# A recurrent attention step and a gated two-layer product on one core: four f-tiles in three passes, paired gates, a step's decays as products, another order

## The chip, the cores and the metric

The kernel runs on one core of a Trainium2 chip. The time is that of the device for one execution, in microseconds (us). Five engines run side by side, each through its own list of instructions in order: TensorE (PE, matrix products), VectorE (DVE), ScalarE (ACT), GpSimd (POOL) and SyncE (SP), which mostly issues transfers. They wait for each other by semaphores.

## What is computed

```python
for t in range(S):                      # B, H, S, D = 4, 8, 768, 48
    kt, vt, rt = (k[:, :, t], v[:, :, t], r[:, :, t])
    cur = np.einsum('bhd,bhe->bhde', u[None] * kt, vt)
    y[:, :, t] = np.einsum('bhd,bhde->bhe', rt, state + cur)
    state = w[None, :, :, None] * state + np.einsum('bhd,bhe->bhde', kt, vt)
x = y.transpose(0, 2, 1, 3).reshape(B * S, H * D)      # 3072 tokens x 384
h = x @ w_in                                           # w_in 384 x 2048
g = h * np.tanh(softplus(h))
out = g @ w_out                                        # w_out 2048 x 384
```

All of it is in float32.

## The kernel before

**Attention.** The recurrence is computed in 24 steps. A step takes 64 tokens of two of the four batches, so step s carries on the states of step s - 2. For each step, DVE multiplies r and k by powers of the decay w (`scale`), PE forms the scores within the 64 tokens (`scores`), DVE puts them under a mask (`attend`) into a tile P that holds on its diagonal the sums of r, u and k. PE then forms the outputs from the carried states and from P and v (`rows_y`), and the new states' additions from the keys (`keys`) and v. The states are multiplied by w to the 64th (`w64`) and added to what PE made (`update_state`): one scaling and two additions on DVE, or the scaling on ACT. The sums for the diagonal come from PE for the first steps (`N_SQ`, `N_PE`: two steps in one form, the steps up to the sixth in another, 32 rows each in the trace) and from three DVE instructions over the normal layout of r and k for the others (`dots`).

**The gated product.** Four steps make a group of 512 tokens; there are six groups, 0 to 5. The 2048 inner columns are 16 f-tiles of 128. For each f-tile PE forms `hp` (x times w_in), ACT or DVE copies it out of PSUM into `hb` (`evacuate`), two f-tiles make a batch of 1024 columns, and ACT runs three functions over it (`gate`: sigmoid, arctangent, sine into `fa`). The third needs another table than the first two, so each batch loads a table twice. DVE multiplies `hb` by the result (`mix`). PE multiplies the product with w_out into three accumulators.

**Two forms of a product.** The weights arrive as 64-bit numbers in 16 blocks (`wraw`) and are turned into float32 by one ACT and three DVE instructions each (`convert`). A float32 product in the plain form shows as two rows in the trace. In the other form a number is split into a high and a low part (type fp32r), for weights by `split` (one ACT and one DVE instruction over 768 columns), and three products are formed: high with high, high with low, low with high (`three`). All groups but 0 use three passes throughout. Group 0 uses the plain form until the weights have been split: its w_in tiles are worked in `UNITS`, first four units of two f-tiles for the first 256 tokens (steps 0 and 1), the same four for the other 256, and then f-tiles 8 to 15 one by one over 512 tokens. Only those last eight use three passes (`FROM` = 8), from a split copy of x (`xp`, made by `split_x`). The products with w_out in group 0 read the gated tile `gf` directly, plain, up to f-tile 13.

**What sets the order.** The program keeps a planner (`Flow`). Each piece of work is a generator that yields what it waits for and what it costs on one or several engines; the planner picks, by these costs, by ranks and by a table of numbers (`SHIFT`), the next piece, and so fixes each engine's list and, for pieces that two engines can do, the engine. On the chip each engine then runs its list in order.

Of the kernel before, what the change touches and what calls it, by code (L numbers as in the profile page):

```python
# [10 lines left out]
F32 = mybir.dt.float32  # L11
# [11 lines left out]
NP = H // 2  # L23
C = 128
# [40 lines left out]
N_SQ, N_PE = 2, 6  # L65
OWN = 3
CHECK_AT, CHECK_STEP = 44, 3
DIAG_ACT = (1, 2, 5, 6, 7, 10)
# [8 lines left out]
def first_use(c):  # L77
# [15 lines left out]
PAIRS = ()  # L93
BY_STEP = 0
FROM, FROM2 = 8, 14
X_SPLIT = 5
CONVERT = (639.144, -3157.076, -1693.42, -2376.477)
LAG = 8
AHEAD_LEAST, AHEAD_MOST, DOWN = 1, 8, 3
LO0, HI0, LO1, HI1 = 0.15, 0.5, 0.1, 0.5  # L100
LAT, LAT0 = 0.15, 0.13
WARM0, WARM_MIN, FILL = 10, 0.3, 0.28
# [9 lines left out]
RANK = dict(token_table=-1935.7, keys=466.6, first_state=-1349.0)  # L112
# [8 lines left out]
    attend10=-85.0, attend9=1.0, convert10=-3.0, convert11=-13.0, convert4=-75.0, convert6=70.0, convert8=-31.0,  # L121
    convert9=77.0, diag5=-21.0, dots10=-7.0, evacuate12=54.0, evacuate23=-33.0, evacuate27=-34.0, evacuate4=87.0,
    gate10=-55.0, gate11=-30.0, gate12=-2.0, gate2=-7.0, gate3=-45.0, gate5=17.0, gate9=-81.0, keys10=20.0,
    mix1=23.0, mix3=-52.0, outputs10=-2.0, outputs12=-8.0, outputs13=2.0, outputs4=-2.0, outputs6=-191.0,
    outputs7=15.0, outputs8=11.0, scale10=5.0, scale11=32.0, scale6=-3.0, scale7=-7.0, split13=-88.0,
# [3 lines left out]
class Flow:  # L129
# [127 lines left out]
def rwkv_mish_kernel(ctx, tc, rkT, rkN, vN, wT, w_in, w_out, consts, rkF, vF, wF, uF, outT):  # L257
# [71 lines left out]
    pre = work.tile([128, 2 * KT * 64], F32, name="pre", tag="fa", bufs=1)  # L329
# [453 lines left out]

    def rows_y(s, last):
# [50 lines left out]
        if not last:  # L835
            state_products(s, new_states(ys), False)
# [14 lines left out]
    def outputs(s):  # L851
# [26 lines left out]
        else:  # L878
            more = merged and with_sums(s + 1)
            yield pe(1.45 + 0.65 * merged - 0.4 * last + 0.27 * more, 192 + 64 * merged - 64 * last + 64 * more)  # L880
# [240 lines left out]
    def tile_cost(g, halved=False):  # L1121
        return pe(9 * (T + 33) / 2400, 18) if g else pe(3 * 4 * (T + 3) / 2400, 24 if halved else 12)

    def split_x():

        if FROM >= NF:
            return
# [3 lines left out]
        for k in range(KT):  # L1131
# [511 lines left out]
```

## Time and profile before

| | |
|---|---|
| median of 3 runs | 466.83 us (466.33 to 466.9) |
| profiled execution | 468.58 us, of which the span from the first to the last instruction is 466.7 us |
| PE busy | 455.4 us (98%) |
| DVE busy | 374.6 us (80%) |
| ACT busy | 392.4 us (84%) |
| DMA | 60.1 MB, 129 GB/s in the mean |

A row of the profile is a group of instructions or a single one with its start, its duration and, in brackets, how long its engine stood idle ahead of it and for whom. PE's matmuls overlap: a row of 512 columns is shown with 0.38 us, though the next starts 0.22 us later, so the spacing of starts is what one costs. PEld are the weight loads. DVE and ACT rows overlap by about 0.1 us in the same way.

### The profile page before, as it was taken

Reading aid. Unit: us, or ns where it says so; the run is one execution under the profiler, and the core shown is the slowest. Engines: PE = TensorE matmul, PEld = TensorE weight load, DVE = VectorE, ACT = ScalarE, POOL = GpSimd, SP = SyncE. Lnnn points to the kernel's source line nnn. Section 1 sums busy time; section 2 is a strip of 40 time slices with the busy share of each in tenths; the row PEclk is TensorE's granted clock in tenths of the full one; section 3 lists DMA queues with packets and bytes.
Section 4 is the critical chain, followed back from the end, with each engine's and each line's share of the span. In section 5 each row is a group of like instructions: output and inputs, shape, how many; then the busy total and the mean of one; then the engine's idle time right before and its main releaser. Section 6 shows DMA issues by size and latency. Waiting matters only on the chain.

```text
span 466.7 us, 11536 instructions
## 1 busy us (share of the span) xinstructions
PE 455.4 (98%) x4927; PEld 382.7 (82%) x4927; DVE 374.6 (80%) x594; ACT 392.4 (84%) x505; POOL 4.5 (1%) x31
## 2 busy tenths in 40 slices
PE   9899999999999999999999999999999999999995
PEld 5687888756888888888888888888888888888884
DVE  6899999999898989597986799986799575646661
ACT  5668897999999885897689978799979799989981
POOL 1000000000000000000000000000000000000000
PEclk9999999999999999999999999999999999999998
DMA  8866666612312331315351365242445040212001
GB/s 313 301 217 217 234 233 215 223 26 95 103 69 91 101 106 44 103 72 164 126 185 67 113 213 202 92 165 69 156 145 194 14 139 22 115 67 70 1 0 72
DMA packets 20168, 60.14 MB, mean 129 GB/s; under 512 B 3312, under 2 KB 4304, under 8 KB 20112
## 3 DMA queue, kind: packets, MB, share of 16 engines
q1 hardware_dynamic: 17664, 55.11, 34.9%
q10 hardware_dynamic: 2448, 4.25, 2.4%
q8 instruction: 39, 0.64, 0.6%
q14 instruction: 17, 0.14, 0.1%
HBM read 52.57 MB, written 4.72 MB: 123 GB/s over the span
## 4 chain that ended last, share of the span: by engine, by line
PE 57%; DVE 14%; DMA 12%; ACT 11%; SPq 2%; issue 2%; ACTq 0%; DVEq 0%
PE acc L360 27%; PE hp L360 27%; DMA wraw<-in_w_out_dram 5%; DMA wraw<-in_w_in_dram 3%; PE pa L360 2%; DMA first<-in_rkT_dram 2%; SPq L988 2%; ACT L1056 2%; DMA kn<-in_rkN_dram 2%; ACT fa L1056 1%; ACT fa L1062 1%; DVE hb L1072 1%; DVE gl L1080 1%; DVE rk L628 1%; ACT L1062 1%
## 5 line engine op out<-in xcount | busy, mean ns | idle before, releaser
L360 PE MATMUL hp<-x,w 128*128 128x512 f32 x720 | 164.8, 382 | 2.0 <-DVE hb L1265 1.5
L360 PEld LDWEIGHTS hp<-x,w 128*128 128x128 f32 x720 | 134.9, 189 | 22.4 <-DVE hb L1265 1.9
L360 PE MATMUL acc<-gh,w 128*128 128x512 f32 x492 | 152.8, 380 | 0.0
L360 PEld LDWEIGHTS acc<-gh,w 128*128 128x128 f32 x492 | 93.0, 189 | 13.5
L360 PE MATMUL acc<-gl,w 128*128 128x512 f32 x246 | 92.7, 379 | 0.0
L1072 DVE TENSOR_TENSOR hb<-hb,fa 128x1024 f32<-128x1024 f32 x40 | 48.9, 1222 | 33.9 <-ACT fa L1062 33.7
L1056 ACT ACT_TABLE_LOAD x47 | 60.3, 1283 | 15.2 <-DVE hb L1072 13.3
L1062 ACT ACT_TABLE_LOAD x47 | 60.3, 1283 | 1.0 <-issue 0.2
L1056 ACT ACTIVATE fa<-hb,small 128x1024 f32<-128x1024 f32 x48 | 55.3, 1152 | 1.6 <-DVE hb L1072 1.0
L1265 DVE COPY hb<-hp 128x512 f32<-128x512 f32 x58 | 39.8, 686 | 17.4 <-PE hp L360 17.2
L360 PEld LDWEIGHTS acc<-gl,w 128*128 128x128 f32 x246 | 46.5, 189 | 6.6
L1059 ACT ACTIVATE fa<-fa 128x1024 f32<-128x1024 f32 x48 | 50.8, 1058 | 0.7
L1062 ACT ACTIVATE fa<-fa 128x1024 f32<-128x1024 f32 x47 | 49.7, 1058 | 0.5
L1080 DVE TENSOR_TENSOR gl<-hb,gh 128x1024 fp32r<-128x1024 f32 x40 | 48.8, 1219 | 1.4 <-ACT gh L1076 1.0
L360 PE MATMUL acc<-gf,wraw 128*128 128x256 f32 (+1 forms) x132 | 38.2, 440 | 0.9 <-PE hp L360 0.8
L360 PEld LDWEIGHTS acc<-gf,wraw 128*128 128x128 f32 x132 | 25.6, 196 | 10.9 <-issue 6.0
L1265 ACT COPY hb<-hp 128x512 f32<-128x512 f32 x38 | 22.0, 581 | 14.1 <-PE hp L360 13.8
L628 DVE TENSOR_TENSOR rk<-rk,TR 112x1024 f32<-112x1024 f32 x22 | 26.8, 1220 | 2.0 <-DMA rk<-in_rkT_dram 1.8
L1076 DVE CAST gh<-hb 128x1024 fp32r<-128x1024 f32 x34 | 23.4, 689 | 3.0 <-PE acc L360 1.8
L360 PE MATMUL hp<-x,wraw 128*128 128x256 f32 x96 | 22.4, 386 | 0.0
L360 PEld LDWEIGHTS hp<-x,wraw 128*128 128x128 f32 x96 | 18.4, 196 | 2.0
L492 ACT ACTIVATE wraw<-wraw 128x768 f32<-128x768 uint32 x16 | 15.5, 978 | 5.3 <-DMA wraw<-in_w_out_dram 3.3
(147 smaller groups left out, 555.5 us busy)
## 6 DMA issues: line engine op xcount, KB each, us to landing
wraw<-in_w_in_dram SPq DMA_DIRECT2D x16, 768.0 KB, 5.3
wraw<-in_w_out_dram SPq DMA_DIRECT2D x16, 768.0 KB, 4.8
rk<-in_rkT_dram SPq DMA_DIRECT2D x22, 512.0 KB, 4.2
rkn<-in_rkN_dram SPq DMA_DIRECT2D x18, 384.0 KB, 4.6
v<-in_vN_dram SPq DMA_DIRECT2D x22, 256.0 KB, 5.0
out_dram<-ob ACTq DMA_DIRECT2D x10, 256.0 KB, 2.1
x<-x SPq DMA_DIRECT2D x60, 32.0 KB, 2.0
out_dram<-we ACTq DMA_DIRECT2D x6, 256.0 KB, 3.1
```

What stands on the lines that cost most here:

```text
L360: ins = nc.tensor.matmul(out, lhsT=lhsT, rhs=rhs, **flags)
L492: nc.scalar.activation(r, low, AF.Copy, bias=2.0, scale=2.0**-51)
L628: nc.vector.tensor_tensor(out=ab, in0=ab, in1=TR[:112].unsqueeze(1).broadcast_to([112, 4, NP, CK]), op=ALU.mult)
L988: nc.sync.dma_start(x[o + D : o + 64, k, b - 1 : b + 1].bitcast(F32).rearrange("e b a t -> e (b a t)"), x[o + 16 * k : o + 16 * k + 16, KT ...
L1056: nc.scalar.activation(o.g, o.hb, AF.Sigmoid, bias=bias_ln2, scale=1.0)
L1059: nc.scalar.activation(o.g, o.g, AF.Arctan)
L1062: nc.scalar.activation(o.g, o.g, AF.Sin, scale=2.0)
L1072: nc.vector.tensor_tensor(out=o.hb, in0=o.hb, in1=o.g, op=ALU.mult)
L1076: (nc.scalar.copy if engine == "act" else nc.vector.tensor_copy)(out=o.gh, in_=o.hb)
L1080: nc.vector.tensor_tensor(out=o.gl, in0=o.hb, in1=o.gh.bitcast(F32), op=ALU.subtract)
L1265: (nc.scalar.copy if engine == "act" else nc.vector.tensor_copy)(out=to, in_=h)
```

## The change

`FROM` goes from 8 to 4: the four f-tiles 4 to 7 of w_in in group 0 also use three passes. They are still worked by halves of the tokens, so a unit is 36 rows of 256 columns for two f-tiles where it was 12. For this, x is split by halves as well (`split_x(h)`, two pieces over three k-tiles each), `xp` has another layout, and the splits of weight blocks 2 and 3 of w_in come ahead of the units that use them. `N_PE` goes from 6 to 4: the sums of steps 4 and 5 are made by DVE. `N_DEC` = 3 lets step 2 form its decayed state as products (`decays`: the states times the diagonal matrices `dw` of w64, into the same accumulator as the new keys), after which the state is a copy. `PAIRS` = (14, 16, 18) runs the gates of batches 14 and 15, 16 and 17, 18 and 19 together, so that one table load serves two batches (batch b holds f-tiles of group b // 8). `DIAG_ACT` names the steps whose diagonal ACT makes. The early loads have another order, and the planner's numbers and its table are others.

```diff
-N_SQ, N_PE = 2, 6
+N_DEC = 3
+N_SQ, N_PE = 2, 4
-DIAG_ACT = (1, 2, 5, 6, 7, 10)
+DIAG_ACT = (0, 1, 2, 5, 9, 10, 11)
 FIRST = (
-    ("rk", 0), ("rk", 1), ("raw", 0), ("v", 0), ("rk", 2), ("rkn", 2), ("raw", 1), ("v", 1), ("v", 2), ("rkn", 1),
-    ("v", 3), ("rkn", 3), ("rkn", 0), ("rk", 3),
+    ("rk", 0), ("rk", 1), ("raw", 0), ("rkn", 2), ("rk", 2), ("v", 0), ("raw", 1), ("rkn", 0), ("v", 1), ("rkn", 3),
+    ("rk", 3), ("v", 2), ("v", 3), ("rkn", 1),
 )
-PAIRS = ()
+PAIRS = (14, 16, 18)
-FROM, FROM2 = 8, 14
-X_SPLIT = 5
+FROM, FROM2 = 4, 14
+X_SPLIT = 4
 SHIFT = dict(
-    attend10=-85.0, attend9=1.0, convert10=-3.0, convert11=-13.0, convert4=-75.0, convert6=70.0, convert8=-31.0,
+    attend10=3.0, attend3=250.0, attend7=-114.0, attend8=194.0, convert10=22.0, convert13=4.0, convert15=-0.4,
...
+    def decayed(s):
+        return 2 <= s < min(N_DEC, NS - 2)
...
+        def decays(cross):
+            new = new_states(ys)
+            for p in range(NP):
+                for i in range(2):
+                    b = i ^ cross
+                    ins = matmul(
+                        new[b][ROWS[i], p], lhsT=dw[ROWS[i], p, i], rhs=states[ROWS[i], 2 * (s % 2) + b, p, :D],
+                        start=False, stop=False,
+                    )
+                    done.append(ins)
...
     def update_state(s, new):
         S = states[r112, s % 2 * 2 : s % 2 * 2 + 2, :, :D]
+        if decayed(s):
+            for b in range(2):
+                engine = yield {**act(192), **dve(192)}
+                (nc.scalar.copy if engine == "act" else nc.vector.tensor_copy)(out=S[:, b], in_=new[b][r112])
...
-        for s in range(B):
-            yield f"x{s}"
-        x_parts.append(work.tile([128, 2, KT, T], F32R, name="xp", tag="xp", bufs=1))
...
+        hs = slice(0, B) if h is None else slice(2 * h, 2 * h + 2)
+        for t in range(hs.start, hs.stop):
+            yield f"x{t}"
+        if not x_parts:
+            x_parts.append(work.tile([128, KT, B, 2, C], F32R, name="xp", tag="xp", bufs=1))
...
+    def three_passes(n):
+        h, c = UNITS[n]
+        return (c if h is None else WG * c) >= FROM
...
+            for i in range(1 if h is None else WG):
+                f = c % WG if h is None else i
+                at, steps = (slice(0, T), slice(0, B)) if h is None else (slice(i * HT, (i + 1) * HT), slice(2 * h, 2 * h + 2))
+                for k in range(KT):
+                    fs = slice((k * WG + f) * 128, (k * WG + f + 1) * 128)
+                    xh, xl = (xp[:, k, steps, j].rearrange("p (q a) t -> p q t a", a=2) for j in range(2))
+                    three(hp[:, at], w[:, 0, fs], w[:, 1, fs], xh, xl, k == 0, k == KT - 1)
```

Three places of the order follow. In it each line is one instruction or a run of equal ones (xN); L is the line of the kernel, and a plain product is one instruction here where the trace shows two rows.

PE, from the outputs of step 3 on, before (`x_261` is x of group 0, `wraw` a converted weight block, `gf` a gated batch, `acc_...` the accumulators):

```order
L360 MATMUL hp<-x_261,wraw 128x256 x6
L360 MATMUL acc_629<-gf,wraw 128x256 x2
L360 MATMUL acc_632<-gf,wraw 128x256 x2
L360 MATMUL acc_635<-gf,wraw 128x256 x2
L360 MATMUL pa<-cst,q 64x1 x16
L360 MATMUL pa<-rk 64x64 x16
L360 MATMUL hp<-x_261,wraw 128x256 x12
```

and after:

```order
L369 MATMUL hp<-xp,w 128x256 x18
L369 MATMUL acc_668<-gf,wraw 128x256 x2
L369 MATMUL acc_671<-gf,wraw 128x256 x2
L369 MATMUL acc_674<-gf,wraw 128x256 x2
L369 MATMUL hp<-xp,w 128x256 x18
L369 MATMUL pa<-rk 64x64 x16
L369 MATMUL hp<-x_274,wraw 128x256 x12
```

The plain unit ahead of the first `gf` products is now one in three passes, a second such unit stands behind them, and step 4's sums (`pa<-cst,q`) are gone.

DVE, around the first product with a gate (`gf`), before (`we` and `wraw` belong to a weight block's conversion):

```order
L975 COPY x_261<-hp 128x2x64
L909 TENSOR_TENSOR S<-S,small 112x8x48
L502 ISA wraw<-wraw,we 128x768x2
L914 TENSOR_TENSOR S<-S,hp 112x4x48
L1070 TENSOR_TENSOR gf<-hb,fa 128x1024
L914 TENSOR_TENSOR S<-S,yt 112x4x48
L632 TENSOR_TENSOR q<-rk 112x2x4x64
L628 TENSOR_TENSOR rk<-rk,TR 112x1024
```

and after (`w` is the low part of a split weight block, `rkn` and `sd` belong to step 4's sums):

```order
L528 TENSOR_TENSOR w<-wraw,w 128x768
L504 TENSOR_SCALAR we<-wraw 128x768
L1104 TENSOR_TENSOR gf<-hb,fa 128x1024
L1009 COPY x_274<-yt 128x2x64
L506 SCALAR_TENSOR_TENSOR we<-wraw,we 128x768
L948 TENSOR_TENSOR S<-S,hp 112x4x48
L510 ISA wraw<-wraw,we 128x768x2
L948 TENSOR_TENSOR S<-S,yt 112x4x48
L682 TENSOR_TENSOR rkn<-rkn,un 128x384
L528 TENSOR_TENSOR w<-wraw,w 128x768
L684 TENSOR_TENSOR rkn<-rkn 128x384
L636 TENSOR_TENSOR rk<-rk,TR 112x1024
```

Two splits of weight blocks now stand around the first `gf`, the second of them ahead of step 4's scaling, and step 4's sums stand on DVE in place of the product q for PE.

ACT, the gates of batches 14 and 15, before (batch 14 here):

```order
L1056 ACT_TABLE_LOAD
L1056 ACTIVATE fa<-hb,small 128x1024
L1265 COPY hb<-hp 128x512
L1059 ACTIVATE fa<-fa 128x1024
L1265 COPY hb<-hp 128x512
L1062 ACT_TABLE_LOAD
L1062 ACTIVATE fa<-fa 128x1024
```

and after (both; `ga` is the second batch's tile):

```order
L1090 ACT_TABLE_LOAD
L1090 ACTIVATE fa<-hb,small 128x1024
L1093 ACTIVATE fa<-fa 128x1024
L1090 ACTIVATE ga<-hb,small 128x1024
L1093 ACTIVATE ga<-ga 128x1024
L1096 ACT_TABLE_LOAD
L1096 ACTIVATE fa<-fa 128x1024
L1096 ACTIVATE ga<-ga 128x1024
```

Two batches share two table loads where each had two of its own.

## Rows read from the trace of the kernel before

**Rows 1.** Busy time by stretch: length, then PE, PEld, DVE, ACT, POOL, clock, DMA
```profile
80.00:105.40 25.40, 24.78 (x207) 16.35 (x205) 24.60 (x40) 25.20 (x41) 0.13 (x2) 1.00 0.41 143
...
126.00:206.00 80.00, 79.10 (x957) 68.41 (x956) 69.76 (x108) 68.55 (x87) 0.44 (x5) 1.00 0.26 85
206.00:286.00 80.00, 78.59 (x957) 68.06 (x956) 65.87 (x109) 66.21 (x79) 0.45 (x5) 1.00 0.44 144
```
**Rows 2.** Waits of DVE from 36.3 to 105.4 us: total, times, longest
```profile
DVE x L978 <- ACT x L975: 1.0, 2, 0.5
DVE P L695 <- ACT sd L668: 0.8, 1, 0.8
DVE we L496 <- DMA wraw<-in_w_out_dram: 0.5, 1, 0.5
DVE gf L1070 <- ACT fa L1062: 0.3, 1, 0.3
DVE xp L1136 <- ACT xp L1134: 0.2, 1, 0.2
```
**Rows 3.** Timeline: start, duration, engine, instruction, idle before (DVE and PE)
```profile
18.89 0.69 DVE L632 TENSOR_TENSOR q<-first 112x512 f32<-112x512 f32 x1 [1.31 <-DMA first<-in_rkT_dram]
...
35.19 1.21 DVE L1070 TENSOR_TENSOR gf<-hb,fa 128x1024 f32<-128x1024 f32 x1
...
102.97 7.89 PE L360 MATMUL acc<-gf,wraw 128*128 128x512 f32 x18
...
104.14 1.23 DVE L1070 TENSOR_TENSOR gf<-hb,fa 128x1024 f32<-128x1024 f32 x1 [0.27 <-ACT fa L1062]
```
**Rows 4.** Timeline of PE and its loads: a plain half unit, and three-pass products
```profile
28.20 2.87 PE L360 MATMUL hp<-x,wraw 128*128 128x256 f32 x12
...
199.98 0.38 PE L360 MATMUL acc<-gl,w 128*128 128x512 f32 x1
199.98 0.41 PEld L360 LDWEIGHTS acc<-gh,w 128*128 128x128 f32 x2
200.20 0.59 PE L360 MATMUL acc<-gh,w 128*128 128x512 f32 x2
```
**Rows 5.** Timeline of PEld: seven loads whose matmuls have two columns
```profile
8.64 0.86 PEld L360 LDWEIGHTS yt<-cst,q 112*128 112x128 f32 x7
```
**Rows 6.** Timeline of PE: a step's sums, its scores, and what follows
```profile
22.49 0.64 PE L360 MATMUL pa<-cst,q 48*64 48x1 f32 x32
22.98 0.67 PE L360 MATMUL pa<-first 48*64 48x64 f32 x32
23.49 0.25 PE L360 MATMUL pb<-v,kn 64*48 64x48 f32 x2
```
**Rows 7.** Timeline of DVE: spacing of rows of 384, 512, 768 and 1024 columns
```profile
61.08 0.54 DVE L674 TENSOR_TENSOR rkn<-rkn,un 128x384 f32<-128x384 f32 x1
61.54 0.68 DVE L1136 TENSOR_TENSOR xp<-x,xp 128x512 fp32r<-128x512 f32 x1
62.14 0.55 DVE L676 TENSOR_TENSOR rkn<-rkn 128x384 f32<-128x384 f32 x1
...
70.65 0.95 DVE L498 SCALAR_TENSOR_TENSOR we<-wraw,we 128x768 uint32<-128x768 uint32 x1
71.51 1.22 DVE L628 TENSOR_TENSOR rk<-rk,TR 112x1024 f32<-112x1024 f32 x1
72.65 0.41 DVE L978 TENSOR_TENSOR x<-pa,x 128x256 fp32r<-128x256 f32 x1
```
**Rows 8.** Waits of PE from 105.6 to 461 us: total, times, longest
```profile
PE hp L360 <- DVE hb L1265: 1.5, 3, 1.0
PE pa L360 <- DVE rk L628: 0.6, 1, 0.6
PE hp L360 <- DVE S L914: 0.4, 1, 0.4
```
**Rows 9.** Costliest groups of ACT: busy us, mean ns, idle before
```profile
L1062 ACT ACT_TABLE_LOAD x47 | 60.3, 1283 | 1.0 <-issue 0.2
```

More of the change, by code (lines that the diff above doesn't have):

```diff
@@ L835, in rows_y @@
         if not last:
+            if decayed(s):
+                decays(0)
             state_products(s, new_states(ys), False)
@@ L879, in outputs @@
             more = merged and with_sums(s + 1)
-            yield pe(1.45 + 0.65 * merged - 0.4 * last + 0.27 * more, 192 + 64 * merged - 64 * last + 64 * more)
+            yield pe(1.45 + 0.65 * merged - 0.4 * last + 0.27 * more + 0.18 * decayed(s), 192 + 64 * (merged - last + more + decayed(s)))
             yield from hp_free(0.0)
@@ L903, in update_state @@
         S = states[r112, s % 2 * 2 : s % 2 * 2 + 2, :, :D]
+        if decayed(s):
+            for b in range(2):
+                engine = yield {**act(192), **dve(192)}
+                (nc.scalar.copy if engine == "act" else nc.vector.tensor_copy)(out=S[:, b], in_=new[b][r112])
+                if not b:
+                    read(s)
+            flow.set(f"state{s}")
+            return
         engine = yield {**dve(384), "act": 0.78}
@@ L1147, in up_unit @@
             return hp
-        if h is None and c >= FROM:
-            w, xp = parts[0, c // WG], x_parts[0]
-            for k in range(KT):
-                fs = slice((k * WG + c % WG) * 128, (k * WG + c % WG + 1) * 128)
-                three(hp, w[:, 0, fs], w[:, 1, fs], woven(xp[:, 0, k]), woven(xp[:, 1, k]), k == 0, k == KT - 1)
+        if three_passes(n):
+            w, xp = parts[0, c // WG if h is None else c], x_parts[0]
+            for i in range(1 if h is None else WG):
[5 more added lines that the diff above has]
+                    three(hp[:, at], w[:, 0, fs], w[:, 1, fs], xh, xl, k == 0, k == KT - 1)
             return hp
@@ L1239, in up_tile @@
                 yield f"x{s}"
-            three_pass = h is None and c >= FROM
+            three_pass = three_passes(n)
             if three_pass:
-                yield "parts"
+                for k in range(2) if h is None else (h,):
+                    yield f"parts{k}"
             c = c if h is not None else c // WG
@@ L1250, in up_tile @@
         yield from hp_free()
-        yield tile_cost(g or three_pass, not g and UNITS[n][0] is not None)
+        yield tile_cost(g or three_pass, not g and h is not None)
         yield from hp_free(0.0)
@@ L1431, in rwkv_mish_kernel @@
     flow.start(check_range(), 999, 0.0)
-    flow.start(split_x(), X_SPLIT, 0.0, "split_x")
+    for h in range(2) if FROM < WG * AHEAD else (None,):
+        flow.start(split_x(h), X_SPLIT, 0.0, f"split_x{'' if h is None else h}")
     flow.start(load_rest(), -1200, 0.0)
```

66 lines of the change are left out of this document (35 added, 31 removed).

## The prediction

> **What bounds the kernel now.** I began with the busy time by stretch [rows 1]. The granted clock is 1.00 throughout, so TensorE (PE) runs at 2.4 GHz and the clock is no part of this change. From 126 to 286 us PE is busy 79.1 and 78.6 of 80 us, VectorE (DVE) 70 and 66: there PE sets the time and the others have room. From 80 to 105.4 us it is different. DVE is busy 24.6 of 25.4 us, ScalarE (ACT) 25.2, PE 24.8. All three are full, and a saving on one engine is worth something only if the others keep up.
>
> So I looked at who waits in the first group. DVE, from the first product with a gate (`gf`, 35.19 us) to the seventh (104.14 us), waits 1.0 + 0.8 + 0.5 + 0.3 + 0.2 = 2.8 us in all [rows 2, 3]; the other 66.2 of these 69.0 us are its own rows. PE begins its run of 18 `gf` rows at 102.97, 0.43 us each, and the seventh row is the first that reads the seventh `gf`: 102.97 + 6 x 0.43 = 105.55 us, 0.2 us after that `gf` is written (104.14 + 1.23) [rows 3]. The two engines come to this place together. I take it as the landmark. In both orders the same PE work stands ahead of it: all sixteen first-matrix tiles of group 0, the second-matrix products of f-tiles 0 to 11, steps 0 to 7.
>
> **The change on PE.** (1) Four f-tiles leave the fp32 form. A half unit of 12 rows takes 2.87 us, a spacing of 0.216 us after the tail of the last row (0.38) and the exposed first load (0.11) are taken off [rows 4]. The four f-tiles are four such units, 48 rows, 10.4 us. After the change they are 72 rows of 256 columns in one pass. No such row is in the trace. Its streaming is half of 0.216, 0.108 us. Its weight load, 128 columns, sets the spacing where matmuls have only two columns: (0.86 - 0.19) / 6 = 0.112 us [rows 5]. In the 512-column products the next load starts at 199.98, with the running matmul, and ends at 200.17, ahead of the matmul at 200.20 [rows 4]. If that holds for short rows, the spacing is the larger of the two, 0.112 us, and 72 rows are 8.1 us: 2.3 us less. In series it would be 0.22 us, 15.8 us: 5.5 us more. I take the overlap, since the load at 199.98 is a full 128 x 128 one of the same type. (2) Steps 4 and 5 lose their sums: 32 rows each, 22.49 to 22.98, so 2 x 0.49 = 1.0 us less [rows 6]. (3) Step 2's decays are 32 small rows; 32 such rows take 22.98 to 23.49, so 0.5 us more [rows 6]. Sum: 2.8 us less on PE, all of it ahead of the landmark. Behind it the PE work is the same.
>
> The Trainium skill speaks against (1): "TensorE: Matmul & The Clock Gate", Part 3, says that a weight load overlaps a running matmul only when the two use different row groups, and ours use all rows. By that the four f-tiles would cost the 15.8 us of the series case; the load at 199.98 in rows 4 shows otherwise for 512 columns, and the case stands below as a rival.
>
> **The change on DVE.** Row spacing is 0.46 us for 384 columns, 0.60 for 512, 0.86 for 768, 1.14 for 1024 [rows 7]. I counted the rows ahead of the seventh `gf` in both orders. More: two splits of weight blocks (2 x 0.86), three steps' sums by the normal layout (9 x 0.46), one scale (1.14), one diagonal (0.60). Less: two products q (2 x 0.60), four evacuations of `hp` that ACT now makes (4 x 0.60), one mask and one key product (0.60 + 0.46). State rows, the split of x in two pieces instead of three and a copy change it by 0.2. That is 7.6 - 4.7 + 0.2, about 3.2 us more. Ahead of the first `gf` the same count gives 1.8 us less: a weight block's two long rows, an evacuation, a diagonal and some state rows have moved behind it, one split and one x split ahead. So between the two marks DVE has 5.0 us more: 66.2 + 5.0 = 71.2 us of rows.
>
> When does the first `gf` start? By rows 1.8 us earlier, 33.4. One wait of 1.31 us for the r and k of step 3 [rows 3] should shrink, since that load is no longer the last of the early ones; against it v of step 0 is loaded behind two more tiles, and the state copies now stand behind two units on PE. I let these cancel: 33.3, with 32.5 and 34.5 as ends. The waits on the way: the 0.8 us for sums `sd` falls, since DVE makes them itself now; the others may stay or go, 0.3 to 2.8 us, and I take 1.0, as DVE now has more queued in front of each. The seventh `gf` starts at 33.3 + 71.2 + 1.0 = 105.5, ends 104.0 to 108.5, against 104.14. PE can pass the landmark at 105.5 + 1.2 + 0.2 = 106.9. By its own work it would be there at 105.55 - 2.8 = 102.75. **DVE comes last: the landmark is 1.35 us later, and PE's saving is spent waiting there.**
>
> **Behind the landmark.** In the whole program DVE loses four evacuations, two copies of results, two casts, a diagonal and two products q (11 x 0.60), three state scalings (3 x 0.46) and two state additions (estimate from rows 7: 0.26 each), 8.5 us; it gains two steps' sums (6 x 0.46), four state copies (4 x 0.26) and a small copy, 4.0. That is 4.5 us less, so 7.7 us less from the landmark on. The three pairs save six table loads, 6 x 1.28 = 7.7 us of ACT [rows 9], about what it takes over from DVE. PE is the bound here, and what can be won is its waits: 1.5 us for evacuations, 0.6 for `rk`, 0.4 for the state, 2.5 us [rows 8]. A DVE with 7.7 us less to do should remove some; a pair holds back its first gate by two passes of ACT, which could add some. Between nothing and all 2.5, I take 1.5 us. ACT's work ahead of the seventh gate is unchanged within 0.1 us, so it is not what comes last at the landmark.
>
> Sum: +1.35 - 1.5 = -0.15 us. The profiled execution's time is 468.58 us over a span of 466.7; the same on the median of the runs, 466.83, gives 466.7.
>
> **Rivals.**
> A, the forecast: DVE decides the first group and later waits give it back. 466.7, own range 465.0 to 468.3.
> B: PE's saving shows. DVE's 69.0 us between the marks are 63.7 by the spacings of rows 7, 2.8 of waits, and 2.5 by which its rows are longer than there. If that stretch came from what ran beside them, it may be smaller in the new order; without it and with 0.3 us of waits the seventh `gf` starts at 102.3 and PE passes the landmark at 103.7, 1.85 us early. With 1 us less waiting later that is 464.0, without 465.0; I write 464.4. For it: nothing in the trace ties the stretch to this work. Against: DVE was as full before.
> C: the first group locks on DVE. The outputs of steps 2 and 3 now follow each other on PE with no unit between them, then PE needs the split of the third weight block; each waits for DVE. If DVE's waits stay at the 2.8 us of rows 2 and the first `gf` is not early (34.5), the seventh starts at 108.5 and the landmark is 4.3 us late; 1.5 us of later gain leave +2.8: 469.6. It decides from a seventh `gf` later than 106.5.
> D: load and matmul go in series (or the change to three passes saves nothing on halves). The 72 rows cost 7.7 us more than I count. PE would reach the landmark at 110.5 by its own work, 5 us late; less 1.5: 470.3.
>
> **How the numbers follow.** Chances: A 0.50, B 0.24, C 0.16, D 0.10. A measurement of this kernel can tell about 0.2% from no change, 0.93 us: faster is under 465.9, slower over 467.8. A puts 0.13 under, 0.29 between, 0.08 over; B is faster but for 0.01; C gives 0.03 to no change; the rest of C and D is slower. So faster 0.36, same 0.33, slower 0.31. The predicted time is A's, 466.7. The range reaches into B and C until 2 in 10 are out: 463.9 to 469.8.
>
> **What would show it.** The 256-column `hp<-xp` rows at 0.11 us spacing, a unit in about 2.0 us (D: 0.22, 4 us). No 64x1 rows for steps 4 and 5. The seventh `gf` on DVE at 105 to 106 us with DVE waits under 2 us since the first, and PE waiting for it or for the sixth by 2 to 4 us, where before it waited under 0.2. Behind 106 us PE's waits for evacuations under 1.5 us, 90 table loads for 96. I am wrong if the landmark lies before 104 us (B) or after 108 (C, D), or if the waits behind it grow.

## The result and the profile after

The changed kernel is slower by 0.7%: median 470.73 us against 466.87 in 20 runs each, ratio 1.0070 (95% interval 1.0054 to 1.0086). Measured again on two other chips, beside the kernel before, it gave 1.0039 (1.0018 to 1.0061) and 1.0053 (1.0031 to 1.0076): slower each time, by 0.4 to 0.7%. 466.7 was forecast, with 469.8 as the upper end. The profiled execution took 470.24 us over a span of 468.5.

The busy time by stretch, with the columns of [rows 1]; first two stretches of the kernel before, then the changed kernel:

```profile
10.00:20.00 10.00, 9.02 (x229) 6.06 (x227) 8.35 (x13) 5.91 (x22) 0.00 (x0) 1.00 1.03 379
30.00:40.00 10.00, 9.05 (x173) 7.32 (x176) 9.91 (x18) 7.55 (x10) 0.32 (x1) 1.00 0.49 163
```
```profile
10.00:20.00 10.00, 8.28 (x213) 5.16 (x214) 8.56 (x13) 5.93 (x20) 0.00 (x0) 0.83 0.94 368
30.00:40.00 10.00, 8.28 (x206) 7.89 (x195) 9.44 (x18) 6.06 (x11) 0.09 (x1) 0.83 0.67 235
80.00:105.40 25.40, 23.50 (x205) 15.63 (x202) 25.40 (x42) 22.95 (x29) 0.13 (x2) 1.00 0.59 195
126.00:206.00 80.00, 79.12 (x985) 68.50 (x977) 69.41 (x109) 67.80 (x95) 0.45 (x5) 1.00 0.28 89
206.00:286.00 80.00, 80.00 (x868) 69.74 (x858) 66.82 (x110) 61.47 (x78) 0.36 (x4) 1.00 0.44 142
```

From 80 to 105.4 us DVE is now full (25.40 of 25.4) and PE is not (23.50 for 24.78). And twice early the granted clock is 0.83 in the mean of ten us, that is, for a third of them at 1.2 GHz; before it was 1.00. PE's longest waits up to 106 us (total, times, longest):

```profile
PE yt L369 <- DVE P L762: 1.7, 1, 1.7
PE yt L369 <- DVE S L933: 1.7, 1, 1.7
PE acc L369 <- DVE gf L1104: 1.6, 1, 1.6
PE pa L369 <- issue: 1.2, 1, 1.2
PE pa L369 <- DVE TR L313: 0.9, 1, 0.9
PE hp L369 <- DVE S L948: 0.9, 1, 0.9
```

The first is at the start of the kernel. DVE's and PE's rows there:

```profile
11.52 0.21 DVE L872 COPY pre<-v 128x96 f32<-128x96 f32 x1 [1.00 <-DMA v<-in_vN_dram]
11.66 0.72 DVE L762 COPY_PREDICATED P<-cst,pa 128x512 f32<-128x512 uint32 x1
...
21.48 1.50 DVE L715 TENSOR_TENSOR kn<-kn,TKn 128x384 f32<-128x384 f32 x3 [1.91 <-ACT TKn L362]
```
```profile
12.44 0.27 PE L369 MATMUL yt<-P,v 64*64 64x64 f32 x1 [1.73 <-DVE P L762]
...
13.59 3.88 PE L369 MATMUL idle<-zeros 128*128 128x512 bf16 x11
```

The mask of step 0 (`P`) stands on DVE behind a copy that waits for v of step 0, which now is loaded behind two more tiles. PE waits for the mask, then its clock falls: eleven idle products that took 2.80 us take 3.88. The table `TKn`, which ACT copies from a product of PE, comes late, and DVE waits 1.91 us for that. This start is one execution's: two later traces of the same kernel (`control` and `control_2` below) have a clock of 1.00 from 10 to 20 us and a wait for `TKn` of 0.2 us or none. The second wait, for the state of step 2 (`S` L933) at 31 us, stands where the plain half unit of [rows 4] filled the time between the outputs of steps 2 and 3. This wait (2.1 and 1.5 us in those two traces) and the third (1.85 and 1.90) are in all three. The third is the one that decides. DVE's gated batches one, six and seven, and PE's rows that read the last two:

```profile
34.39 1.22 DVE L1104 TENSOR_TENSOR gf<-hb,fa 128x1024 f32<-128x1024 f32 x1
...
98.60 1.32 DVE L1104 TENSOR_TENSOR gf<-hb,fa 128x1024 f32<-128x1024 f32 x1
...
107.08 1.32 DVE L1104 TENSOR_TENSOR gf<-hb,fa 128x1024 f32<-128x1024 f32 x1
```
```profile
99.98 5.43 PE L369 MATMUL acc<-gf,wraw 128*128 128x512 f32 x12 [1.57 <-DVE gf L1104]
104.84 4.45 PE L369 MATMUL hp<-xp,w 128*128 128x512 f32 x18
109.13 2.74 PE L369 MATMUL acc<-gf,wraw 128*128 128x512 f32 x6
```

And the same place before (the row at 102.97 is in [rows 3]):

```profile
95.13 5.65 PE L360 MATMUL acc<-gf,wraw 128*128 128x512 f32 x12
100.93 2.21 PE L360 MATMUL hp<-xp,w 128*128 128x512 f32 x9
```
```profile
96.60 1.28 DVE L1070 TENSOR_TENSOR gf<-hb,fa 128x1024 f32<-128x1024 f32 x1
```

Before, PE came to its first row with the sixth batch (the seventh of the 12 rows at 95.13: 97.93 us) 0.05 us after DVE had written it, so it did not wait. After, it waits 1.57 us for the sixth and comes there at 99.98, 2.05 us later. From there it has 9.15 us of its own to the landmark (the first row with the seventh, 109.13), where it had 7.62. The landmark is 3.58 us late, against 1.35 in the forecast.

### The profile page after: what moved, and what is told of

Same layout as the page of the kernel before. It is cut to its first block, busy times and chain, and to the rows that moved or that the text cites. A ratio compares the mean times of both kernels' runs of the same rounds, so it can differ in the third digit from the quotient of the medians.

```text
span 468.5 us, 11531 instructions
## 1 busy us (share of the span) xinstructions
PE 454.0 (97%) x4919; PEld 383.7 (82%) x4919; DVE 369.9 (79%) x588; ACT 393.7 (84%) x517; POOL 4.2 (1%) x31
## 4 chain that ended last, share of the span: by engine, by line
PE 64%; DVE 14%; ACT 10%; DMA 7%; issue 3%; SPq 2%; ACTq 0%; DVEq 0%
PE acc L369 30%; PE hp L369 29%; DMA wraw<-in_w_out_dram 3%; PE pa L369 2%; ACT w L526 2%; DVE we L506 2%; DVE wraw L510 2%; DMA v<-in_vN_dram 2%; DMA rkn<-in_rkN_dram 2%; DVE gf L1104 1%; ACT L1090 1%; PE yt L369 1%; DVE w L528 1%; ACT fa L1090 1%; ACT L1096 1%
## 5 line engine op out<-in xcount | busy, mean ns | idle before, releaser
L1106 DVE TENSOR_TENSOR hb<-hb,fa 128x1024 f32<-128x1024 f32 x37 | 45.2, 1221 | 39.1 <-ACT fa L1096 39.0
L1090 ACT ACTIVATE fa<-hb,small 128x1024 f32<-128x1024 f32 x45 | 51.8, 1150 | 2.3 <-DVE hb L1106 1.8
L1308 DVE COPY hb<-hp 128x512 f32<-128x512 f32 x54 | 37.1, 686 | 15.8 <-PE hp L369 15.5
L1093 ACT ACTIVATE fa<-fa 128x1024 f32<-128x1024 f32 x45 | 47.6, 1059 | 0.9
L1096 ACT ACTIVATE fa<-fa 128x1024 f32<-128x1024 f32 x44 | 46.6, 1059 | 0.5
L1308 ACT COPY hb<-hp 128x512 f32<-128x512 f32 x42 | 24.3, 582 | 16.5 <-PE hp L369 15.6
L369 PEld LDWEIGHTS acc<-gf,wraw 128*128 128x128 f32 x132 | 25.4, 196 | 10.4 <-issue 6.0
L369 PE MATMUL hp<-xp,w 128*128 128x256 f32 (+1 forms) x144 | 27.5, 346 | 1.2 <-DVE S L948 0.9
L369 PEld LDWEIGHTS hp<-xp,w 128*128 128x128 f32 x144 | 22.6, 197 | 4.7 <-DVE S L948 1.1
L1110 DVE CAST gh<-hb 128x1024 fp32r<-128x1024 f32 x32 | 22.0, 688 | 3.1 <-PE acc L369 2.0
L447 ACT ACTIVATE we<-wraw 128x768 f32<-128x768 f32 x16 | 19.0, 1187 | 0.6 <-DMA wraw<-in_w_in_dram 0.4
```

Of the source, the lines that this page charges most:

```text
L369: ins = nc.tensor.matmul(out, lhsT=lhsT, rhs=rhs, **flags)
L447: nc.scalar.activation(e, raw[:, :, 1].bitcast(F32), AF.Square, accum_out=to[:, 1:2])
L1090: nc.scalar.activation(o.g, o.hb, AF.Sigmoid, bias=bias_ln2, scale=1.0)
L1093: nc.scalar.activation(o.g, o.g, AF.Arctan)
L1096: nc.scalar.activation(o.g, o.g, AF.Sin, scale=2.0)
L1106: nc.vector.tensor_tensor(out=o.hb, in0=o.hb, in1=o.g, op=ALU.mult)
```

## The experiments

All kernels but the three under "Parts undone" keep every engine's list as in the changed kernel except for the edit. `control` and `control_2` are the changed kernel itself, on two other chips. The table puts the traces side by side: start of the first and sixth gated batch on DVE, landmark on PE, the profiled execution's time and what of it lies behind the landmark, and the median of the runs with the ratio to the kernel before.

| kernel | first | sixth | landmark | profiled | behind | median | ratio (95%) |
|---|---|---|---|---|---|---|---|
| before | 35.2 | 96.6 | 105.55 | 468.58 | 363.03 | 466.87 | 1 |
| changed | 34.4 | 98.6 | 109.13 | 470.24 | 361.11 | 470.73 | 1.0070 (1.0054-1.0086) |
| v0_early | 32.5 | 97.9 | 108.35 | 469.57 | 361.22 | 469.37 | 1.0058 (1.0036-1.0081) |
| idle_out0 | 33.3 | 97.8 | 108.18 | 469.35 | 361.17 | 469.58 | 1.0066 (1.0042-1.0090) |
| idle_out3 | 32.7 | 97.2 | 107.63 | 468.53 | 360.90 | 468.60 | 1.0033 (1.0010-1.0055) |
| v0_idle3 | 32.5 | 96.2 | 106.66 | 467.76 | 361.10 | 467.70 | 1.0022 (0.9998-1.0045) |
| dve_less | 33.6 | 98.5 | 110.64 | 471.98 | 361.34 | 470.24 | 1.0067 (1.0044-1.0091) |
| loads_free | 32.8 | 99.8 | 110.21 | 471.07 | 360.86 | 470.93 | 1.0074 (1.0045-1.0102) |
| loads_free_dve_less | 32.7 | 98.4 | 108.77 | 470.21 | 361.44 | 469.88 | 1.0050 (1.0032-1.0068) |
| pe_less | 32.0 | 98.8 | 109.25 | 472.11 | 362.86 | 469.63 | 1.0048 (1.0025-1.0071) |
| pe_dve_less | 32.7 | 98.0 | 108.44 | 470.37 | 361.93 | 470.38 | 1.0051 (1.0031-1.0071) |
| control | 33.1 | 98.2 | 110.26 | 471.49 | 361.23 | 469.22 | 1.0039 (1.0018-1.0061) |
| no_pairs | 32.8 | 98.9 | 111.05 | 471.60 | 360.55 | 469.05 | 1.0036 (1.0020-1.0053) |
| v0_idle3_no_pairs | 34.3 | 99.1 | 111.25 | 471.73 | 360.48 | 467.96 | 1.0019 (0.9993-1.0044) |
| raw10_early | 31.9 | 96.3 | 106.78 | 467.89 | 361.11 | 468.26 | 1.0019 (1.0005-1.0034) |
| raw10_early_dve_less | 32.7 | 98.7 | 109.18 | 470.29 | 361.11 | 468.39 | 1.0018 (1.0001-1.0036) |
| npe6_v0_idle3 | 32.3 | 95.6 | 107.48 | 468.68 | 361.20 | 469.14 | 1.0046 (1.0030-1.0063) |
| clock_only | 33.3 | 97.6 | 108.05 | 469.31 | 361.26 | 469.11 | 1.0046 (1.0019-1.0073) |
| control_2 | 32.9 | 98.2 | 108.62 | 469.58 | 360.96 | 469.56 | 1.0053 (1.0031-1.0076) |
| v0_idle3_2 | 32.1 | 96.5 | 106.96 | 468.15 | 361.19 | 468.44 | 1.0039 (1.0013-1.0064) |

These shared a chip, each group with the kernel before, whose median there follows: v0_early to idle_out3 with dve_less (467.14); v0_idle3 with loads_free, loads_free_dve_less and no_pairs (467.20); pe_less, pe_dve_less, control and v0_idle3_no_pairs (466.87); the three with raw10 or npe6 (467.70); the last three (467.67). The expectations were written against the 470.73 of the first chip. The changed kernel gave 1.5 and 1.2 us less on two others (control was expected at 470.2 at least), so a variant is compared with control and control_2 by its ratio or its trace, and a difference under 1.5 us between two chips shows nothing by itself.

### The late start and the clock

`v0_early`, shown as the change in the order of the early loads (cut):

```diff
-    ("rk", 0), ("rk", 1), ("raw", 0), ("rkn", 2), ("rk", 2), ("v", 0), ("raw", 1), ...
+    ("rk", 0), ("rk", 1), ("raw", 0), ("v", 0), ("rkn", 2), ("rk", 2), ("raw", 1), ...
```

> The changed kernel with one move on SP alone: the load of v of step 0 is issued third after rk 0, rk 1 and the first weight block, as in the kernel before, instead of behind two more tiles; every other engine's list is unchanged. In the changed kernel DVE waits 1.00 us for this v at 11.52 us, the mask of step 0 stands behind that copy, PE waits 1.7 us for the mask (10.5 to 12.4 us) and its granted clock is 0.50 from 13 to 16 us; the table TKn then comes late and DVE waits 1.91 us for it at 21.48. Theory 1 (DVE decides the first group, and is late because of this start): PE's wait for the mask under 0.5 us, clock 1.00 in 10 to 20 us, the wait for TKn nearly gone, the first gated product on DVE at 32.5 to 33.2 us instead of 34.4, the seventh at 105.2 to 105.9 instead of 107.1, the time 1.2 to 1.9 us less than the changed kernel: 468.8 to 469.5, still above the 466.9 of the kernel before. Theory 2 (PE's own waits and its low clock are the loss): the 1.9 us of wait and some 1.6 us of half clock both come back, 467.2. Rival (the start is hidden behind what DVE does later): 470.7, no change.

Measured 469.37. PE's wait for the mask was 0.5 us, the clock 1.00 in 10 to 20 us, the wait for `TKn` gone, the first batch at 32.5: as theory 1 said. The sixth came only 0.7 us earlier, since now ACT and the natural r and k held DVE up by 0.9 and 1.2 us. But control and control_2, where v is still late, have the first batch at 33.1 and 32.9 and the sixth at 98.2, and the ratio, 1.0058, lies between theirs and 1.0070: no gain from an early v alone is shown.

`idle_out0`, and `idle_out3` with 3 for 0:

```diff
+    for _ in range({0: 8}.get(s, 0)):
+        matmul(idle, lhsT=z.broadcast_to([128, 128]), rhs=z.broadcast_to([128, 512]), start=True, stop=True)
     ys = spread_y(s)        # rows_y(s, last) for step 3
```

> The changed kernel with eight idle products of 512 columns (0.216 us each) put ahead of the outputs of step 0, in the 1.9 us in which PE waits for the mask; nothing else moves. It holds the wait and takes away only the fall of the clock that follows it. Theory 1: clock 1.00 in 10 to 20 us, the outputs of step 1 at 15.8 us instead of 17.4, the wait of DVE for TKn 0.3 instead of 1.9 us, first gated product at 32.8, time 1.3 to 1.6 us less, 469.1 to 469.4. Theory 2 gives the same here, 469.1. Rival (the start is hidden): 470.7.

> The changed kernel with eight idle products ahead of the outputs of step 3, in the 1.9 us in which PE waits for the state of step 2 (31.0 to 32.9 us); nothing else moves. In the changed kernel the granted clock is 0.50 from 34 to 36 us behind this wait. Theory 1 (DVE decides the first group; from 34.4 to 108 us it waits for PE nowhere): the clock is 1.00 there, PE is 1.6 us earlier at 37 us, and waits that much longer for the sixth or the seventh gated product: 470.4 to 470.9, no change. Theory 2 (PE's waits and clock are the loss): 1.6 us less, 469.1.

Measured 469.58 and 468.60 on one chip. By its ratio, 1.0066, idle_out0 gains nothing. idle_out3 looked like theory 2, 2.1 us below the changed kernel's median of the first chip. But its trace has the first batch at 32.7, ahead of the place where it could help, and against control and control_2 it is only 0.6 and 1.0 us less.

`v0_idle3` is both edits.

> Both mends that helped alone: v of step 0 loaded third (alone 469.37 against 470.73 of the changed kernel) and eight idle products in PE's wait ahead of the outputs of step 3 (alone 468.60). Found so far: in every profiled run of the changed kernel and its variants the last product with weights starts 363.1 to 363.4 us after the first product that reads the sixth gated batch, and that one waits 1.5 to 2.5 us for DVE; so what moves the sixth gated batch moves the end. Theory S (the loss is the late start and the low clock behind two waits of PE, which delay the transfers of x at 33 to 37 us on SP and all that is queued there behind them): the two gains add, clock 0.997 to 1.00 in all executions, the first gated product at 32.0 to 32.6 us, the sixth at 96.5 to 97.0 instead of 98.6, time 466.9 to 467.6, within 0.2% of the kernel before. Theory D (the rows of DVE decide by themselves): they do not add, 468.4 to 469.0, DVE busy 20.0 of 20 us from 80 to 100.

467.70, 0.1 us above the range of theory S, with the sixth batch at 96.24, a little earlier than that theory had it. Its rows on DVE and PE:

```profile
32.54 1.22 DVE L1115 TENSOR_TENSOR gf<-hb,fa 128x1024 f32<-128x1024 f32 x1
...
96.24 1.22 DVE L1115 TENSOR_TENSOR gf<-hb,fa 128x1024 f32<-128x1024 f32 x1
```
```profile
97.52 5.42 PE L373 MATMUL acc<-gf,wraw 128*128 128x512 f32 x12 [1.58 <-DVE gf L1115]
102.38 4.45 PE L373 MATMUL hp<-xp,w 128*128 128x512 f32 x18
106.66 2.74 PE L373 MATMUL acc<-gf,wraw 128*128 128x512 f32 x6
```

Even so PE waits 1.58 us for the sixth. The next three ran on one chip. `clock_only` has both sets of idle products and the late v; `control_2` is the changed kernel, `v0_idle3_2` the mended one, with both edits.

> The changed kernel with eight idle products ahead of the outputs of step 0 and eight ahead of the outputs of step 3: both waits of PE stay, both falls of the clock go. Beside the changed kernel on the same chip. If the low clock itself is the loss: clock 0.997 to 1.00 in all executions and 1.5 to 2.5 us less than the changed kernel. If the waits are, and the low clock only shows them: no more than 0.5 us less.

> The changed kernel itself on the same chip: 469.2 to 470.8, clock 0.990 to 0.995.

> The mended version (v of step 0 third, eight idle products ahead of the outputs of step 3) on the same chip as the changed kernel. If late start and low clock are the part of the loss that shows: 1.5 to 2.5 us less than the changed kernel beside it and 0.3 to 1.2 us more than the kernel before. If the two kernels differed only by their chips so far: within 0.5 us of the changed kernel.

The clock of clock_only in the two stretches was 1.00 (columns as above), and yet it measured 469.11 against 469.56 of control_2, whose trace has 1.00 and 0.66 there:

```profile
10.00:20.00 10.00, 10.00 (x234) 6.28 (x233) 8.73 (x13) 6.98 (x25) 0.00 (x0) 1.00 1.02 370
30.00:40.00 10.00, 8.51 (x139) 6.99 (x138) 10.00 (x20) 5.88 (x12) 0.09 (x1) 1.00 0.67 227
```

By this pair the low clock ahead of 40 us costs about 0.5 us or nothing. Another pair says more: v0_early and v0_idle3 differ by the eight idle products ahead of step 3 alone, the clock from 30 to 40 us is 0.66 in one and 1.00 in the other, and with the same first batch (32.5) the sixth is 1.7 us apart and the ratio 1.0058 against 1.0022. These two ran on different chips, so the cost of that low clock stays open between nothing and 1.7 us. The mended version is 1.1 us below the changed one on the same chip; its two ratios are 1.0022 and 1.0039, those of the changed kernel 1.0039 to 1.0070. Their intervals overlap, so this size rests on the traces (landmark 1.7 us earlier on that chip) as much as on the times.

### Rows left out on DVE and on PE

`dve_less` leaves out one row (the sign bit) of two weight blocks' conversions:

```diff
-        marks[f"bent{c}"] = v.scalar_tensor_tensor(
+        if c not in (8, 9):
+            marks[f"bent{c}"] = v.scalar_tensor_tensor(
```

> The changed kernel without two of DVE's rows: the middle row (the sign bit) of the conversion of the ninth and tenth weight blocks is left out, at about 59 and 71 us, 0.86 us each by spacing. All other lists are unchanged. Theory 1 (DVE decides the first group): the sixth and the seventh gated product come 1.7 us earlier (96.9 and 105.4), PE's wait of 1.6 us for the sixth is gone, time 1.4 to 1.7 us less, 469.0 to 469.3. Theory 2 (PE's own lateness decides): PE's wait moves elsewhere or stays, 470.4 to 470.9.

470.24, ratio 1.0067: no gain, and the sixth batch at 98.5 beside 98.2 in both controls, so theory 1 in its plain form fell. DVE's and ACT's rows show what filled the hole:

```profile
71.68 1.23 DVE L1105 TENSOR_TENSOR gf<-hb,fa 128x1024 f32<-128x1024 f32 x1 [1.01 <-ACT fa L1097]
96.85 0.42 DVE L1013 TENSOR_TENSOR x<-pa,x 128x256 fp32r<-128x256 f32 x1 [1.25 <-ACT x L1010]
```
```profile
95.30 1.26 ACT L500 ACTIVATE wraw<-wraw 128x768 f32<-128x768 uint32 x1 [2.36 <-DMA wraw<-in_w_out_dram]
```

DVE now waits 1.0 us for a gate on ACT and 1.25 for ACT's part of x, which stands behind a weight block that landed at 95.3. To part these, `loads_free` drops the rule of one weight block at a time, and the next kernel adds dve_less:

```diff
-            if before:
+            if False:
                 tc.add_manual_dep(ins.ins, before.ins.name, sync, ...)
```

> The changed kernel without the rule that one weight block is under way at a time: SP issues the next block when its turn in the list comes, not when the block ahead has landed. No list changes. In the changed kernel ACT begins the last conversions ahead of the sixth gated batch at 93.0 to 97.0 us, with no wait for a block, and DVE's rows follow each other from 60 to 99 us. Theory D: no gain, 470.2 to 471.0. Theory W (the chain of weight blocks behind the transfers of x decides): blocks land 2 us and more earlier after 73 us, the sixth gated batch at 97.0 or earlier, 469.0 or less. Against both: more transfers at once lengthen the loads of r and k, for which DVE waits 1.5 us now, and the time grows.

> The same with two of DVE's rows left out (the sign bit in the conversion of the ninth and tenth weight blocks, 0.86 us each). With the rows left out alone the time was 470.24, no gain, and in that trace ACT waited 2.4 us for the weight block that landed at 95.3 us, whose conversion DVE makes right ahead of the sixth gated batch. If the chain of weight blocks is what stood behind DVE's rows there, both together bring what neither does alone: no wait for that block, the sixth gated batch at 96.8 to 97.4 instead of 98.5, 468.9 to 469.5. If not (PE or ACT stands behind them), 470.2 to 470.8.

470.93, as theory D had it, and 469.88, between the two cases: the waits for blocks are gone, the 1.0 us for the gate stays, and PE's idle time ahead of `pa` for which the profile shows no releaser (the row "issue") was 4.0 and 2.8 us in these traces against 1.2 to 2.0 in the three of the changed kernel. Here, with the blocks out of the way and on one chip, the rows left out on DVE brought 1.05 us in the median and 1.44 at the landmark; the intervals of the two ratios overlap, and neither kernel is faster than the changed one.

`pe_less` leaves out 24 rows of PE (in the half units it drops the part of the product with the low half of x), `pe_dve_less` both; `control` ran beside them.

```diff
-                    three(hp[:, at], w[:, 0, fs], w[:, 1, fs], xh, xl, k == 0, k == KT - 1)
+                    if h is None:
+                        three(hp[:, at], w[:, 0, fs], w[:, 1, fs], xh, xl, k == 0, k == KT - 1)
+                        continue
+                    matmul(hp[:, at], lhsT=w[:, 0, fs], rhs=xh, start=k == 0, stop=False)
+                    matmul(hp[:, at], lhsT=w[:, 1, fs], rhs=xh, start=False, stop=k == KT - 1)
```

> The changed kernel without the middle product (high part of the weights with low part of x) of the four three-pass half units of group 0: 24 rows of 256 columns at 0.112 us, 2.7 us of PE at 35 to 56 us. All other lists are unchanged. Found so far: leaving out 1.7 us of DVE's rows brought nothing clear (470.24 against 470.73), while mending PE's late start and its low clock brought 3.0 us (467.7). Theory S (PE's lateness is what the first group pays): 1.0 to 2.7 us less, 468.0 to 469.7, the sixth gated batch at 96 to 97.5 us. Theory D (DVE's rows decide): PE waits 2.7 us longer, 470.4 to 471.0. Theory T (PE, ACT and DVE tie, each as late as the next): less than 0.7 us, 470.0 to 470.7.

> Both left out, the 24 rows of PE and the two rows of DVE. Theory S: as without the rows of PE alone. Theory D: as without the rows of DVE alone, 469.9 to 470.3. Theory T: what neither brings alone, 1.2 to 1.7 us less than the changed kernel, 469.0 to 469.5.

> The changed kernel itself, on the same chip as the other three of this call, since clock and times of one kernel differ a little between chips. 470.2 to 471.2.

469.63 and 470.38. By its number pe_less falls into the range of theory S, but control, on the same chip, measured 469.22, 1.0 us under its own range: neither engine's rows left out alone, nor both, brought anything. In pe_less DVE waits 2.1 us for ACT's x, in pe_dve_less 1.9.

`raw10_early` issues a weight block ahead of the transfers of x in the mended version, so that the chain of blocks has no hole; the second kernel adds dve_less. The edit, cut:

```diff
         yield {"sp": 3.6}
+        if s == 5:
+            load_weight(10)
```

> The version with v of step 0 third and eight idle products (467.7), and the load of the eleventh weight block issued on SP ahead of the transfers of x of steps 4 and 5 instead of behind them; nothing else moves. In the traces of the changed kernel the block ahead of it is issued at 64.0 us and this one at 73.2, though a block takes 4 to 7 us: SP is at the transfers of x from 67.5 us. The last four blocks follow one by one, and in six of the variants ACT waits 1.4 to 3.1 us for the last, which lands at 94.6 to 95.7 us; DVE then waits up to 2.1 us for ACT, and the sixth gated batch starts at 98.0 to 98.9. Theory W (behind DVE's rows the last weight block decides): the last block is issued by 86 us and lands by 91, ACT waits for no block from 76 us on, the sixth gated batch 42.0 to 42.4 us after the second, and the slower executions go: median 466.9 to 467.5, mean under 467.7. If not W: 467.7 to 468.2.

> The same with two of DVE's rows left out (the sign bit in the conversion of the ninth and tenth weight blocks, 0.86 us each, at about 57 and 69 us). With the weight blocks out of the way, theory D+W (DVE's rows and the weight blocks are the two that decide the sixth gated batch): it starts 40.4 to 41.0 us after the second instead of 42.3, and the time is 1.2 to 1.7 us less than the version beside it, 465.4 to 466.2. If PE or the gates on ACT stand right behind: no more than 0.5 us less.

468.26 and 468.39. From 41 us on ACT waits for no block, as theory W asked, but the sixth batch is where the mended version has it (96.3), and the rows left out on DVE again bring nothing. In the second trace DVE waits 2.41 us for r and k ahead of the first row left out, which makes that execution late, and 0.98 for a gate behind it, where raw10_early has no wait for a gate:

```profile
47.63 1.22 DVE L647 TENSOR_TENSOR rk<-rk,TR 112x1024 f32<-112x1024 f32 x1 [2.41 <-DMA rk<-in_rkT_dram]
...
71.77 1.23 DVE L1124 TENSOR_TENSOR gf<-hb,fa 128x1024 f32<-128x1024 f32 x1 [0.98 <-ACT fa L1116]
```

### Parts undone

`no_pairs` and `v0_idle3_no_pairs` (in the second with the mend), and `npe6_v0_idle3`, which is planned anew:

```diff
-PAIRS = (14, 16, 18)
+PAIRS = ()
```
```diff
-N_SQ, N_PE = 2, 4
+N_SQ, N_PE = 2, 6
```

> The changed kernel with PAIRS empty: batches 14 to 19 have two table loads each again (94 table loads instead of 88). Lists are the same up to batch 14; behind it a short piece of each is in another order. If the pairs give back part of the 1.8 us that the changed kernel gains behind the first group: 0.3 to 1.2 us slower than the changed kernel, 471.0 to 471.9. If they are off the path: 470.5 to 470.9.

> The version with v of step 0 loaded third and eight idle products ahead of the outputs of step 3 (467.7), and PAIRS empty. In the traces the last product with weights starts 354.1 us after the first product that reads the seventh gated batch with the pairs, 353.5 without, and without them the changed kernel measured 469.05. If the pairs cost on the path, 0.5 to 1.2 us less than 467.7: 466.5 to 467.2, level with the kernel before. If the difference was the clock of those runs alone, 467.5 to 468.0.

> One part undone in the mended version (467.7): N_PE is 6 again, so the sums of steps 4 and 5 are made by PE (32 small rows each, 0.5 us) and DVE has two products of 0.60 us for six rows of 0.46, 1.6 us less; the order is planned anew with the two shifts on these sums taken out. DVE's wait for the natural r and k of steps 4 and 5 (1.5 us in the changed kernel) goes. If DVE's rows decide the first group: 0.8 to 1.6 us less, 466.1 to 466.9. If not: 467.7 to 468.7, since PE has 1.0 us more.

Without the pairs the ratios are 1.0036 and 1.0019, level with 1.0039 (control) and 1.0022 (v0_idle3) with them. no_pairs was expected at 470.5 at least and gave 469.05: that expectation, too, was written against 470.73. Behind the landmark their two traces have 360.5 us, the others with pairs mostly 361.1: the pairs give nothing back that shows, and cost perhaps 0.6 us. With N_PE = 6 the sixth batch is earliest of all (95.6), but the seventh, in this order 10.7 us behind it, holds the landmark at 107.48; 469.14, above both ranges. The three passes themselves, the decays and the planner's other numbers were not undone one by one, so which of them makes the first group longer is not shown.

## Why the forecast was wrong, step by step

The step that failed is the first term of the sum, +1.35 us at the landmark. It measured 3.07 to 4.71 us in the three traces of the changed kernel, by the forecast's own sign of being wrong (a landmark after 108). In the forecast's terms:

| | first batch | DVE's rows | DVE's waits | seventh batch | from it to the landmark | landmark | shift |
|---|---|---|---|---|---|---|---|
| forecast | 33.3 | 71.2 | 1.0 | 105.5 | 1.4 | 106.9 | +1.35 |
| changed | 34.39 | 71.2 | 1.5 | 107.08 | 2.05 | 109.13 | +3.58 |
| control | 33.13 | 71.5 | 2.0 | 106.64 | 3.62 | 110.26 | +4.71 |
| control_2 | 32.86 | 71.3 | 2.5 | 106.69 | 1.93 | 108.62 | +3.07 |

The rows of the two controls, first and seventh batch, and what DVE waited for between them, control first:

```profile
33.13 1.22 DVE L1104 TENSOR_TENSOR gf<-hb,fa 128x1024 f32<-128x1024 f32 x1
106.64 1.20 DVE L1104 TENSOR_TENSOR gf<-hb,fa 128x1024 f32<-128x1024 f32 x1
...
DVE rk L636 <- DMA rk<-in_rkT_dram: 1.8, 1, 1.8
```
```profile
32.86 1.22 DVE L1104 TENSOR_TENSOR gf<-hb,fa 128x1024 f32<-128x1024 f32 x1
106.69 1.21 DVE L1104 TENSOR_TENSOR gf<-hb,fa 128x1024 f32<-128x1024 f32 x1
...
DVE rk L636 <- DMA rk<-in_rkT_dram: 2.0, 1, 2.0
```

**PE's rows, right.** A half unit in three passes (PE's row, after) has 18 rows, not the 36 that "The change" gives:

```profile
50.74 2.27 PE L369 MATMUL hp<-xp,w 128*128 128x256 f32 x18
```

Less the 0.38 of the last row that is 0.11 us a row: the load goes under the matmul also at 256 columns, and rival D is out. The Trainium skill ("TensorE: Matmul & The Clock Gate", Part 3) states that a load overlaps only where row groups differ; that does not hold here. What PE saved it did not keep: in the first trace its waits up to 106 us are 8.3 us in all, where they were 3.2.

**DVE's rows, right; its start and its waits, not.** From the first batch to the seventh DVE's rows are 71.2 to 71.5 us in the three traces, as forecast. In the first trace the start is 1.1 us late: there "I let these cancel" fails, with v of step 0 worth 1.0 us of DVE's wait, 1.7 of PE's, and 1.9 again for `TKn`. In the two others the start is 0.2 and 0.4 us early, v costs DVE 0.4 and 0.5, and the waits between the marks are 2.0 and 2.5 us in place of 1.0, most of it for one load of r and k. Either way the seventh batch comes 1.1 to 1.6 us late.

**The landmark, in the wrong place.** I asked for the seventh batch, because PE reads it last. In the new order PE waits for the sixth (1.57, 1.85 and 1.90 us), and 18 `hp` rows stand between it and the seventh, 9 before. By the forecast's way PE would follow the seventh after 1.4 us; it takes 1.9 to 3.6, by its own rows from the sixth on (in control at a low clock, last section).

**The late waits, in part open.** PE's waits behind 106 us did shrink, from 2.5 to 1.3 us:

```profile
PE hp L369 <- DVE hb L1308: 0.9, 1, 0.9
PE hp L369 <- ACT hb L1308: 0.4, 1, 0.4
```

and the stretch behind the landmark is 1.9 us shorter than in the profile of before (361.11 for 363.03). On the first chip the median shows none of it: +3.6 at the landmark and nothing back is 470.45; measured 470.73. control_2, whose profiled execution lies at its median, has +3.07 at the landmark and a median 1.89 above that of the kernel before on its chip, so 1.2 us would have come back there. Over all thirteen kernels whose profile lies within 0.5 us of their median, the loss against the kernel before on the same chip is the shift of the landmark less 1.2 us at most and plus 0.6 at most, in eleven of them less than the shift. So of the 1.5 us that I took back from [rows 8], between nothing and 1.2 is seen. The profiled execution of before took 468.58, 1.71 above its kernel's median; I saw that and carried the whole sum over to the median. If the 1.71 lie behind its landmark, part of the 1.5 us was never there to win; if they lie ahead of it, the landmark moved by more than the table says. A second trace of before would tell, and there is none.

**The clock.** "The clock is no part of this change" was wrong as a fact: it falls ahead of 40 us in all three traces of the changed kernel, and what that costs is open, as said above. Rival C was nearest: the seventh batch comes after 106.5, the outputs of steps 2 and 3 do wait (1.5 to 2.1 us), and 469.6 is between the medians. Its reason, DVE alone, is not what the runs show: DVE, ACT's gates, the weight blocks and the loads of r and k arrive close together, and what was taken from one was mostly waited away at another. Open is what would make that group shorter; no version was found that beats the kernel before.

## What to carry to other kernels

Work saved on one engine in a stretch where several are full is worth nothing until the last of them is known, and taking rows out of each in turn is the test. Set a landmark at the first place where an engine waits, not at the last. Take more than one trace of a kernel before you explain its waits: here the late start of the first trace was not in the next two. Before a wait is counted as a gain, ask whether the profiled execution is one of the longer ones of its kernel: what only it shows may not be there to win.

## What was not expected of the hardware

Where the clock falls decides what it costs. In control PE waited 1.85 us for the sixth batch and its clock fell behind it; in control_2, with 1.90 us of wait, it did not. The rows of PE and of the stretch (columns as above), control first:

```profile
99.42 7.12 PE L369 MATMUL acc<-gf,wraw 128*128 128x512 f32 x12 [1.85 <-DVE gf L1104]
105.97 4.45 PE L369 MATMUL hp<-xp,w 128*128 128x512 f32 x18
```
```profile
99.40:104.60 5.20, 5.18 (x8) 2.25 (x9) 5.20 (x8) 5.09 (x5) 0.00 (x0) 0.67 0.27 70
```

and control_2:

```profile
99.47 5.42 PE L369 MATMUL acc<-gf,wraw 128*128 128x512 f32 x12 [1.90 <-DVE gf L1104]
104.33 4.45 PE L369 MATMUL hp<-xp,w 128*128 128x512 f32 x18
```
```profile
99.40:104.60 5.20, 5.13 (x13) 2.46 (x13) 5.20 (x8) 5.03 (x5) 0.00 (x0) 1.00 0.22 71
```

The twelve rows take 6.55 us for 4.86, and all of the 1.69 us shows at the landmark and in the end (471.49 for 469.58): PE has no wait left ahead of the landmark to hide it. Four of the nineteen traces of the changed kernel and its variants have this fall (control, dve_less, no_pairs, v0_idle3_no_pairs: 10.84 us from the sixth batch to the landmark instead of 9.15). Their profiled executions lie 1.7 to 3.8 us above their kernels' medians, so it is likely a part of why executions of one kernel lie some 5 us apart: of v0_idle3_no_pairs ten took 467.46 to 468.84 us at a mean clock of 0.996 to 1.000, and two, the profiled one among them, 471.73 and 472.93 at 0.992 and 0.991.
